# An attention and gated-MLP kernel on one core: the first 180 steps of its hand-written order rearranged

## The chip, the core and the metric

The kernel runs on one core of one Trainium2 chip. A core has five engines that run side by side and meet only at semaphores: TensorE (PE in the profile, with its weight loads as PEld), VectorE (DVE), ScalarE (ACT), GpSimd (POOL) and SyncE (SP). Sixteen DMA engines move data between HBM and the core's memory; SyncE and GpSimd issue the transfers. TensorE writes its results to PSUM, from where VectorE or ScalarE must fetch them. The metric is the device time of one execution in microseconds; less is better.

## The reference

Windowed attention with sink positions (4 batches, 8 heads, 768 positions, head size 64; window 128, 4 sinks), and behind it a gated MLP block on the 512 concatenated features:

```python
scores = scale * np.matmul(q, k.transpose(0, 1, 3, 2))
keep = is_sink | in_window          # pos < 4, or 0 <= i - j < 128
a = softmax(np.where(keep, scores, -1e9))
x = concat_heads(np.matmul(a, v))   # (4, 768, 512)
h = gelu_tanh(x @ w_in)             # 512 -> 1024
u, v = h[..., :512], h[..., 512:]
v_n = (v - mean(v)) / sqrt(var(v) + 1e-6) * g_ln
v_s = einsum('ts,bsd->btd', w_sg, v_n) + b_sg[None, :, None]
out = x + (u * v_s) @ w_out
```

## The kernel before

The four batches go through the same stages, and the stages of neighbouring batches overlap. The order is written out by hand: `STEPS` (lines 20 to 70) is a list of step names, and the loop at line 696 emits them one after another. Each engine runs the instructions it gets from this list strictly in that order. A step that must wait holds up everything behind it on its own engine and nothing on the others. A letter at the end of a step's name says which engine does it: A is ScalarE, D VectorE, P GpSimd, N nobody (the work isn't needed).

The first number of a name is the batch. The steps that matter here, all of batch 0 unless noted:

- LPQ.g, LPK.g (L245 to 253): SyncE loads q or k of two heads (a pair g, 0 to 3) as float32 into tiles that later hold other things (uT and z in the profile's names).
- CPQ.g, CPK.g (L255 to 259, recorded at L200, L201 or L205): cast a pair to bf16.
- TQ, TK (L364 to 377): twelve transposes on TensorE of a pair's q or k into a PSUM tile of the ring mm. EQ, EK (L408 to 432, recorded at L200 or L201): the copy from there to qT or kT.
- QK.0.p.g (L474 to 485): the scores of head pair p and the query blocks 2g and 2g+1, into the ring sc of two tiles. With a 1 at the end, bias matmuls (L479) with -1e9 at the masked places go first, and no mask is needed behind it. EX (L487): exp on ScalarE, from sc to a tile P. MK (L491 to 506): the mask by a multiplication on VectorE, or by two selects on GpSimd; N where the bias was added.
- KS, SK, SX (L450 to 469): the scores of the sinks. KS reads kT of all four pairs.
- LVH.0.0 and LVH.0.1 (L271): GpSimd issues the loads of v for heads 0 to 3 and 4 to 7. ZERO (L347) writes a column of ones into the same tiles beforehand.
- AV.0.p.k (L530 to 554): the products with v for pair p and the query blocks 2k and 2k+1. k = 0 has 6 matmuls, k = 1 and 2 have 10. NR (L556): VectorE divides by the row sums into x_sb, and frees the PSUM tile.
- XT, XE (L565 to 573): transposes of x and their copy to xT. MV, GV, BN, RS, NM, Z (L582 to 621): the half v of the hidden layer, its gelu, statistics and normalised form z. MU, GU: the half u.
- LQ, LK, LW, LWS, LB: further loads that GpSimd issues, of batches 1 and 2 and of the weights. WT, WE: transposes of w_sg and their copy to wsgT.
- SP.0.hf.dc (L644): the products with w_sg, six matmuls that read all of z. GT (L651): VectorE takes their result. VSM (L357), GM (L656) and others stand behind it on VectorE.
- HM.n (L185): n matmuls of zeros (L191) that are put ahead of the next TensorE step which takes a fresh PSUM tile. They keep TensorE busy and compute nothing.

The ring mm has four PSUM tiles, and a step that takes one waits until the copy or division four tiles back has read it. Waits between steps come from the tiles that they share; nothing else sets the order.

Of the kernel before, what the change touches and what calls it, by code (L numbers as in the profile page):

```python
# [17 lines left out]


STEPS = """  # L20
WARM LPQ.0 FILL LPK.0 LPK.1 LPQ.1 LPQ.2 LG MASK LPK.2 LPK.3 CPQ.0.A VSK LPQ.3 IDEN CPK.0.A IDEN2 MASK0 HM.9 TQ.0.0
TK.0.0 EQ.0.0.D EK.0.0.A VSO HM.4 QK.0.0.0 ZERO CPK.1.P QK.0.0.1.1 EX.0.0.0 LVH.0.0 EX.0.0.1 MK.0.0.1.N QK.0.0.2.1
CPQ.1.D TK.0.1 EX.0.0.2 MK.0.0.2.N LC CPQ.2.D LVH.0.1 TQ.0.1 MK.0.0.0.D EK.0.1.A HM.1 TQ.0.2 EQ.0.1.D EQ.0.2.A HM.3
QK.0.1.0 CPK.2.A CPK.3.P QK.0.1.1.1 EX.0.1.0 LQ.1.0 CPQ.3.D TK.0.2 EX.0.1.1 MK.0.1.1.N TK.0.3 EK.0.2.D LQ.1.1 TQ.0.3
EK.0.3.A GTR EQ.0.3.D LW.0 HM.1 QK.0.2.0 QK.0.2.1 EX.0.2.0 LK.1.0 KS.0 VSM.0 HM.3 SK.0.2 EX.0.2.1 SK.0.1 MK.0.2.0.D
AV.0.0.0 LW.1 QK.0.3.0.1 MK.0.1.0.D SX.0.1 SX.0.2 QK.0.3.1 MK.0.2.1.P GCP.D NR.0.0.0 EX.0.3.0 MK.0.3.0.N AV.0.0.1
AV.0.1.0 AV.0.1.1 NR.0.0.1 EX.0.3.1 QK.0.1.2 NR.0.1.0 AV.0.2.0 AV.0.3.0 EX.0.1.2 MK.0.3.1.P NR.0.1.1 QK.0.2.2 AV.0.2.1
NR.0.2.0 EX.0.2.2 TQ.1.0 NR.0.3.0 MK.0.1.2.P QK.0.3.2 AV.0.3.1 EQ.1.0.A NR.0.2.1 XT.0.0 NR.0.3.1 LWS.0 AV.0.0.2
EX.0.3.2 TBL.G.1 AV.0.1.2 XE.0.0.D LK.1.1 XT.0.1 MK.0.2.2.D MV.0.0 XE.0.1.A LK.1.2 NR.0.0.2 MK.0.3.2.D LK.1.3 NR.0.1.2
AV.0.2.2 AV.0.3.2 LQ.1.2 NR.0.2.2 GV.0.0 MV.0.1 NR.0.3.2 LQ.1.3 BN.0.0 LWS.1 XT.0.2 GV.0.1 MU.0.1 XE.0.2.A BN.0.1 WT.0  # L30
GU.0.1 TK.1.0 MV.0.2 LK.1.4 WT.2 EK.1.0.A RS.0.1 LK.1.5 NM.0.1 LB.P LK.2.0 WE.0.D KS.1 GV.0.2 WT.1 MU.0.2 TQ.1.1
LQ.2.0 Z.0.0.D Z.0.3.A Z.0.2.A EQ.1.1.A MU.0.0 WT.5 LQ.2.1 WE.1.D Z.0.1.A BN.0.2 RS.0.2 WE.2.D NM.0.2 GU.0.2 Z.0.4.D
WE.5.D Z.0.5.D TK.1.1 WT.3 EK.1.1.D LQ.1.4 SP.0.0.0 WE.3.D GU.0.0 QK.1.1.0 QK.1.0.0 SP.0.0.2 EX.1.1.0 LQ.1.5 LK.2.1
LVH.1.0 LVH.1.1 GT.0.0.0 TK.1.2 QK.1.2.0 EX.1.0.0 EX.1.2.0 WT.4 GT.0.0.2 SP.0.0.1 EK.1.2.A QK.1.3.0 QK.1.1.1 LQ.2.2
LWO EX.1.3.0 VSM.1 GM.0.0.0.D LK.2.2 GM.0.0.2.P EX.1.1.1 TQ.1.2 WE.4.D SP.0.0.3 TQ.2.0 LK.2.3 QK.1.3.1 LQ.2.3
MK.1.0.0.D GT.0.0.1 MK.1.2.0.D EQ.1.2.A MK.1.3.0.D QK.1.0.1 EX.1.3.1 SP.0.1.1 LQ.2.4 GT.0.0.3 SK.1.0 EX.1.0.1 SX.1.0
LQ.2.5 QK.1.2.1 MK.1.1.1.D MK.1.1.0.D SP.0.1.0 EQ.2.0.D MK.1.3.1.D EX.1.2.1 GM.0.0.3.D TK.2.0 EK.2.0.A GT.0.1.1
QK.1.0.2 QK.1.2.2 SP.0.1.3 GM.0.0.1.D MK.1.0.1.P AV.1.1.0 EX.1.2.2 MK.1.2.1.D GT.0.1.0 GT.0.1.3 LK.2.4 LK.2.5 EX.1.0.2
NR.1.1.0 SP.0.1.2 GT.0.1.2 AV.1.3.0 MK.1.2.2.P QK.1.1.2 NR.1.3.0 AV.1.0.0 OU.0.0 NR.1.0.0 EX.1.1.2 MK.1.0.2.P AV.1.2.0
QK.1.3.2 TK.2.1 MK.1.1.2.P QK.2.1.0 RA.0.0 NR.1.2.0 SN.1.0.1 EX.1.3.2 EX.2.1.0 EK.2.1.D AV.1.0.1 AV.1.2.1 TQ.2.1  # L40
# [695 lines left out]
```

## Time and profile before

| | us |
|---|---|
| median of 3 runs | 155.47 (155.2 to 155.62) |
| the profiled execution | 155.49 |
| its span, first to last instruction | 153.8 |
| TensorE busy | 145.1 |
| VectorE busy | 121.0 |
| GpSimd busy | 103.0 |
| ScalarE busy | 102.9 |

The granted TensorE clock is 1.0 in every slice. A row of the profile names the line, the engine, the operation, what is written from what, the shapes and the count; times are microseconds from the span's start. The list of waits says which engine sat idle before an instruction and what ended it. The chain of waits follows the last instruction back to what released it, step by step. In a row of the order of time, the first number is the start, the second the length.

### The profile page before, as it was taken

What the parts mean: (1) busy time and instruction counts of PE and PEld (TensorE: products, weight loads), DVE (VectorE), ACT (ScalarE), POOL (GpSimd) and SP (SyncE); (2) the same over time, 40 slices, a digit from 0 to 9 for tenths busy, and PEclk for the clock granted to TensorE, in tenths of its full rate; (3) what the DMA queues carried; (4) which work ended last, traced back from release to release, by engine and by line L of the source; (5) the groups of instructions that cost most, each with busy time, mean ns of one, the idle gap of its engine ahead of it and who ended that gap; (6) DMA issues with size and microseconds to landing.
All of it is one profiled execution on the core that took longest, in us unless ns stands there. A gap on an engine that the chain in (4) does not pass through costs nothing.

```text
span 153.8 us, 3859 instructions
## 1 busy us (share of the span) xinstructions
PE 145.1 (94%) x1538; PEld 93.8 (61%) x1554; DVE 121.0 (79%) x291; ACT 102.9 (67%) x119; POOL 103.0 (67%) x134
## 2 busy tenths in 40 slices
PE   6899799999999799999999999999999999999990
PEld 2355476779666577558557664684567644865550
DVE  4677789867899997799969896966889854975982
ACT  3699899588999657767996882578675008597000
POOL 4099689589999979999586947770698900404700
PEclk9999999999999999999999999999999999999999
DMA  4999999999999999999999488999730961064055
GB/s 154 291 376 158 150 197 196 167 188 213 158 150 156 181 152 143 127 150 156 157 216 258 84 272 169 84 231 99 226 119 0 105 124 48 0 205 141 0 205 209
DMA packets 87178, 24.67 MB, mean 160 GB/s; under 512 B 78772, under 2 KB 84920, under 8 KB 87160
## 3 DMA queue, kind: packets, MB, share of 16 engines
q0 software_dynamic: 64608, 11.01, 99.1%
q1 hardware_dynamic: 22552, 13.41, 33.0%
q8 instruction: 12, 0.20, 0.5%
q14 instruction: 6, 0.05, 0.1%
HBM read 24.81 MB, written 6.29 MB: 202 GB/s over the span
## 4 chain that ended last, share of the span: by engine, by line
PE 79%; DMA 9%; DVE 6%; issue 2%; SPq 1%; POOL 1%; DVEq 0%
PE mm L647 18%; PE sc L627 14%; PE sc L586 13%; PE mm L664 13%; DMA v_sb<-in_v_dram 6%; PE sc L484 6%; PE mm L543 5%; DMA uT<-in_k_dram 4%; PE mm L547 3%; DVE P L498 3%; PE mm L383 2%; PE mm L551 1%; DVE gtmp L652 1%; PE mm L639 1%; PE mm L570 1%
## 5 line engine op out<-in xcount | busy, mean ns | idle before, releaser
L489 ACT ACTIVATE P<-sc 128x1024 bf16<-128x1024 f32 (+1 forms) x48 | 43.8, 962 | 11.5 <-PE sc L484 11.0
L647 PE MATMUL mm<-wsgT,z 128*128 128x384 bf16 x192 | 34.5, 326 | 0.9 <-DVE gtmp L652 0.9
L647 PEld LDWEIGHTS <-z 128*128 128x128 bf16 x192 | 17.8, 98 | 12.6 <-issue 1.3
L652 DVE SCALAR_TENSOR_TENSOR gtmp<-mm,g_sb,b_bc 128x384 bf16<-128x384 f32 x32 | 19.1, 611 | 6.1 <-PE mm L647 5.4
L501 POOL TENSOR_SCALAR_AFFINE_SELECT P<-P 128x512 bf16<-128x512 bf16 x23 | 14.9, 648 | 12.7 <-ACT P L489 12.6
L657 POOL TENSOR_TENSOR wsg_gated<-gtmp,uT 128x384 bf16<-128x384 bf16 x18 | 16.5, 931 | 10.1 <-DVE gtmp L652 10.0
L627 PE MATMUL sc<-xT,w_in_sb 128*128 128x256 bf16 x192 | 22.1, 273 | 0.0
L586 PE MATMUL sc<-w_in_sb,xT 128*128 128x512 bf16 x91 | 21.6, 379 | 0.3
L664 PE MATMUL mm<-w_out_sb,wsg_gated 128*128 128x512 bf16 x84 | 21.4, 379 | 0.4
L627 PEld LDWEIGHTS <-w_in_sb 128*128 128x128 bf16 x192 | 18.7, 98 | 3.0
L599 DVE BATCH_NORM_STATS2 st<-vt 128x6 f32<-128x512 f32 x24 | 15.4, 682 | 5.7 <-ACT vt L590 5.6
L561 DVE TENSOR_TENSOR x_sb<-mm,rcp 128x384 bf16<-128x384 f32 (+1 forms) x36 | 18.5, 513 | 1.2
L590 ACT ACTIVATE vt<-sc 128x1024 f32<-128x1024 f32 x12 | 12.3, 1025 | 9.3 <-PE sc L586 9.2
L668 DVE TENSOR_TENSOR ot<-mm,x_sb 128x512 f32<-128x512 f32 x23 | 15.6, 683 | 3.6 <-PE mm L664 3.6
L226 POOL DMA_DIRECT2D k<-in_k_dram x18 | 16.7, 938 | 0.0
L608 POOL TENSOR_TENSOR rs<-rs,neg_half 128x4 f32<-128x4 f32 (+1 forms) x8 | 7.0, 878 | 14.0 <-DVE rs L603 13.1
L226 POOL DMA_DIRECT2D q<-in_q_dram x18 | 16.3, 918 | 0.0
L543 PE MATMUL mm<-v_sb,P 128*128 128x65 bf16 x192 | 15.1, 194 | 1.2 <-DMA v_sb<-in_v_dram 0.8
L543 PEld LDWEIGHTS <-P 128*128 128x128 bf16 x192 | 13.4, 98 | 3.8 <-issue 1.1
L484 PE MATMUL sc<-qT,kT 64*128 64x128 bf16 (+1 forms) x256 | 15.4, 238 | 0.1
L586 PEld LDWEIGHTS <-xT 128*128 128x128 bf16 x96 | 9.3, 98 | 10.3
L504 POOL TENSOR_SCALAR_AFFINE_SELECT P<-P 128x512 bf16<-128x512 bf16 x23 | 15.0, 650 | 0.0
...
## 6 DMA issues: line engine op xcount, KB each, us to landing
...
```

The lines of the kernel that those rows point to most:

```text
L226: return nc.gpsimd.dma_start(out=dst.rearrange("p (h d) -> p h d", h=H), in_=heads(src, b, i))
L484: nc.tensor.matmul(sc[:, hl, c:c + 128 * ni], at(kT, b)[rows, j, p, :], at(qT, b)[rows, i:i + ni, p, :], start=not biased, stop=(not biase ...
L489: nc.scalar.activation(out=P.new((b, p, g))[:, :, 0:w], in_=sc_ring[b, p, g][:, :, 0:w], func=AF.Exp, scale=scale)
L543: nc.tensor.matmul(av[:, il, hl, :], pt[:, hl, c:c + 128], vb[:, h, i, :], start=first, stop=False)
L561: nc.vector.tensor_mul(x_sb.get(b)[:, i0:i0 + n, 128 * p:128 * (p + 1)].rearrange("p t (h d) -> p t h d", h=2), av[:, :, :, 0:Dh], rcp[:, ...
L586: nc.tensor.matmul(hp[:, jl, :], xT[b][:, 2 * g + jl, c, :], w_in_sb[:, c, d_half:2 * d_half], start=(c == 0), stop=(c == KD - 1))
L627: nc.tensor.matmul(hp[:, dc // 2, 256 * (dc % 2):256 * (dc % 2 + 1)], w_in_sb[:, c, 128 * dc:128 * (dc + 1)], xT[b][:, 2 * g:2 * g + 2, c, :],
L647: nc.tensor.matmul(ps[:, 0:NH], z[b][:, si, 128 * dc:128 * (dc + 1)], wsgT[:, si, NH * hf:NH * (hf + 1)], start=(si == 0), stop=(si == NT ...
L652: nc.vector.scalar_tensor_tensor(out=gtmp.new((b, hf, dc)), in0=mm_ring["g", b, hf, dc][:, 0:NH], scalar=g_sb[:, dc:dc + 1], in1=b_bc[:, N ...
L657: (nc.vector if e == "D" else nc.gpsimd).tensor_mul(gated(b, hf)[:, dc, :], gtmp[b, hf, dc], uT[b][:, dc, NH * hf:NH * (hf + 1)])
L664: nc.tensor.matmul(ps, gated(b, hf)[:, dc, 128 * tl:128 * (tl + 1)], w_out_sb[:, dc, :], start=(dc == 0), stop=(dc == KU - 1))
L668: nc.vector.tensor_add(ot.new((b, t)), mm_ring["o", b, t], x_sb[b][:, t, :])
```

## The change

Only the text of `STEPS` changes, and in it only the steps up to the first product with w_sg (SP.0.0.0); from there on the lists are equal. Both hold the same steps of computation. What differs:

- GpSimd's list: LVH.0.0 and LVH.0.1 have no cast ahead of them any more. CPK.2 and CPQ.3 stand between LQ.1.0 and LQ.1.1; before, CPK.1 stood ahead of LVH.0.0 and CPK.3 ahead of LQ.1.0. MK.0.1.2 and MK.0.2.1 leave it and MK.0.3.2 comes. RS.0.2 stands ahead of LQ.2.1 and RS.0.1 behind LK.1.5.
- Casts and copies: CPK.1 and CPQ.1 go to ScalarE, CPK.3 to VectorE, CPK.2 and CPQ.3 to GpSimd. EK.0.0, EK.0.1 and EQ.0.2 go from ScalarE to VectorE, EQ.0.1 to ScalarE.
- Scores: QK.0.0.1 goes ahead of QK.0.0.0. QK.0.3.0 goes ahead of the sink scores and of the first product with v. Biased are QK.0.0.0, 0.0.2, 0.2.1, 0.3.0 and 0.1.2 (before: 0.0.1, 0.0.2, 0.1.1 and 0.3.0).
- Products with v: AV.0.1.0 AV.0.0.0, QK.0.1.2, QK.0.3.1, AV.0.2.0 AV.0.3.0, AV.0.1.1 AV.0.0.1 and so on. Before: AV.0.0.0, QK.0.3.0, QK.0.3.1, AV.0.0.1 AV.0.1.0 AV.0.1.1, QK.0.1.2, AV.0.2.0 AV.0.3.0.
- Warm-up matmuls: 20 instead of 21, at other places.
- Behind that: XE.0.1 and XE.0.2 go from ScalarE to VectorE, Z.0.0 and Z.0.5 the other way, Z.0.2 and EQ.1.1 to VectorE, WE.1 to ScalarE. The transposes WT and TQ.1.1, TK.1.0 stand in another order.

```diff
-WARM LPQ.0 FILL LPK.0 LPK.1 LPQ.1 LPQ.2 LG MASK LPK.2 LPK.3 CPQ.0.A VSK LPQ.3 IDEN CPK.0.A IDEN2 MASK0 HM.9 TQ.0.0
-TK.0.0 EQ.0.0.D EK.0.0.A VSO HM.4 QK.0.0.0 ZERO CPK.1.P QK.0.0.1.1 EX.0.0.0 LVH.0.0 EX.0.0.1 MK.0.0.1.N QK.0.0.2.1
-CPQ.1.D TK.0.1 EX.0.0.2 MK.0.0.2.N LC CPQ.2.D LVH.0.1 TQ.0.1 MK.0.0.0.D EK.0.1.A HM.1 TQ.0.2 EQ.0.1.D EQ.0.2.A HM.3
-QK.0.1.0 CPK.2.A CPK.3.P QK.0.1.1.1 EX.0.1.0 LQ.1.0 CPQ.3.D TK.0.2 EX.0.1.1 MK.0.1.1.N TK.0.3 EK.0.2.D LQ.1.1 TQ.0.3
-EK.0.3.A GTR EQ.0.3.D LW.0 HM.1 QK.0.2.0 QK.0.2.1 EX.0.2.0 LK.1.0 KS.0 VSM.0 HM.3 SK.0.2 EX.0.2.1 SK.0.1 MK.0.2.0.D
-AV.0.0.0 LW.1 QK.0.3.0.1 MK.0.1.0.D SX.0.1 SX.0.2 QK.0.3.1 MK.0.2.1.P GCP.D NR.0.0.0 EX.0.3.0 MK.0.3.0.N AV.0.0.1
-AV.0.1.0 AV.0.1.1 NR.0.0.1 EX.0.3.1 QK.0.1.2 NR.0.1.0 AV.0.2.0 AV.0.3.0 EX.0.1.2 MK.0.3.1.P NR.0.1.1 QK.0.2.2 AV.0.2.1
-NR.0.2.0 EX.0.2.2 TQ.1.0 NR.0.3.0 MK.0.1.2.P QK.0.3.2 AV.0.3.1 EQ.1.0.A NR.0.2.1 XT.0.0 NR.0.3.1 LWS.0 AV.0.0.2
-EX.0.3.2 TBL.G.1 AV.0.1.2 XE.0.0.D LK.1.1 XT.0.1 MK.0.2.2.D MV.0.0 XE.0.1.A LK.1.2 NR.0.0.2 MK.0.3.2.D LK.1.3 NR.0.1.2
-AV.0.2.2 AV.0.3.2 LQ.1.2 NR.0.2.2 GV.0.0 MV.0.1 NR.0.3.2 LQ.1.3 BN.0.0 LWS.1 XT.0.2 GV.0.1 MU.0.1 XE.0.2.A BN.0.1 WT.0
-GU.0.1 TK.1.0 MV.0.2 LK.1.4 WT.2 EK.1.0.A RS.0.1 LK.1.5 NM.0.1 LB.P LK.2.0 WE.0.D KS.1 GV.0.2 WT.1 MU.0.2 TQ.1.1
-LQ.2.0 Z.0.0.D Z.0.3.A Z.0.2.A EQ.1.1.A MU.0.0 WT.5 LQ.2.1 WE.1.D Z.0.1.A BN.0.2 RS.0.2 WE.2.D NM.0.2 GU.0.2 Z.0.4.D
-WE.5.D Z.0.5.D TK.1.1 WT.3 EK.1.1.D LQ.1.4 SP.0.0.0 WE.3.D GU.0.0 QK.1.1.0 QK.1.0.0 SP.0.0.2 EX.1.1.0 LQ.1.5 LK.2.1
-LVH.1.0 LVH.1.1 GT.0.0.0 TK.1.2 QK.1.2.0 EX.1.0.0 EX.1.2.0 WT.4 GT.0.0.2 SP.0.0.1 EK.1.2.A QK.1.3.0 QK.1.1.1 LQ.2.2
-LWO EX.1.3.0 VSM.1 GM.0.0.0.D LK.2.2 GM.0.0.2.P EX.1.1.1 TQ.1.2 WE.4.D SP.0.0.3 TQ.2.0 LK.2.3 QK.1.3.1 LQ.2.3
-MK.1.0.0.D GT.0.0.1 MK.1.2.0.D EQ.1.2.A MK.1.3.0.D QK.1.0.1 EX.1.3.1 SP.0.1.1 LQ.2.4 GT.0.0.3 SK.1.0 EX.1.0.1 SX.1.0
-LQ.2.5 QK.1.2.1 MK.1.1.1.D MK.1.1.0.D SP.0.1.0 EQ.2.0.D MK.1.3.1.D EX.1.2.1 GM.0.0.3.D TK.2.0 EK.2.0.A GT.0.1.1
+WARM LPQ.0 FILL LPK.0 LPK.1 LPQ.1 LPQ.2 LG MASK LPK.2 LPK.3 CPQ.0.A IDEN IDEN2 HM.9 TQ.0.0 MASK0 EQ.0.0.D VSK VSO
+LPQ.3 CPK.0.A ZERO LVH.0.0 HM.3 TK.0.0 LC CPK.1.A EK.0.0.D HM.4 QK.0.0.1 QK.0.0.0.1 EX.0.0.1 LVH.0.1 CPQ.1.A
+MK.0.0.1.D HM.1 TK.0.1 EX.0.0.0 MK.0.0.0.N LQ.1.0 CPK.2.P QK.0.0.2.1 CPQ.3.P EX.0.0.2 CPQ.2.D TQ.0.1 TQ.0.2 TK.0.2
+EQ.0.1.A EK.0.1.D HM.2 QK.0.1.0 LQ.1.1 EQ.0.2.D EX.0.1.0 QK.0.1.1 TQ.0.3 EK.0.2.D CPK.3.D GTR QK.0.2.0 EX.0.1.1
+EX.0.2.0 MK.0.1.0.D LW.0 EQ.0.3.D GCP.D MK.0.1.1.D TK.0.3 EK.0.3.A KS.0 QK.0.2.1.1 EX.0.2.1 QK.0.3.0.1 EX.0.3.0 SK.0.1
+SK.0.2 AV.0.1.0 SX.0.1 MK.0.0.2.N AV.0.0.0 VSM.0 LK.1.0 MK.0.2.0.D QK.0.1.2.1 MK.0.2.1.N SX.0.2 LW.1 QK.0.3.1
+MK.0.3.0.N HM.1 AV.0.2.0 NR.0.1.0 AV.0.3.0 NR.0.0.0 EX.0.3.1 LWS.0 NR.0.2.0 AV.0.1.1 AV.0.0.1 EX.0.1.2 LK.1.1 NR.0.3.0
+TQ.1.0 AV.0.2.1 QK.0.2.2 QK.0.3.2 NR.0.1.1 MK.0.3.1.P AV.0.3.1 NR.0.0.1 NR.0.2.1 NR.0.3.1 XT.0.0 XE.0.0.D EQ.1.0.A
+EX.0.2.2 AV.0.0.2 MK.0.2.2.D MK.0.1.2.N XT.0.1 AV.0.1.2 LK.1.2 MV.0.0 EX.0.3.2 NR.0.1.2 LK.1.3 MK.0.3.2.P NR.0.0.2
+AV.0.2.2 LQ.1.2 LQ.1.3 LWS.1 LK.1.4 TBL.G.1 XE.0.1.D NR.0.2.2 AV.0.3.2 MV.0.1 NR.0.3.2 XT.0.2 GV.0.0 BN.0.0 XE.0.2.D
+MU.0.1 GV.0.1 TK.1.0 BN.0.1 LK.1.5 MV.0.2 GU.0.1 WT.1 RS.0.1 EK.1.0.A NM.0.1 GV.0.2 WE.1.A Z.0.3.A LB.P WT.0 MU.0.2
+Z.0.0.A WT.2 LK.2.0 Z.0.1.A TK.1.1 MU.0.0 TQ.1.1 Z.0.2.D GU.0.2 KS.1 BN.0.2 LQ.2.0 RS.0.2 WE.0.D EK.1.1.D WT.3 WE.2.D
+LQ.2.1 WT.5 NM.0.2 Z.0.5.A Z.0.4.D EQ.1.1.D WE.5.D LQ.1.4 SP.0.0.0 WE.3.D GU.0.0 QK.1.1.0 QK.1.0.0 SP.0.0.2 EX.1.1.0
+LQ.1.5 LK.2.1 LVH.1.0 LVH.1.1 GT.0.0.0 TK.1.2 QK.1.2.0 EX.1.0.0 EX.1.2.0 WT.4 GT.0.0.2 SP.0.0.1 EK.1.2.A QK.1.3.0
+QK.1.1.1 LQ.2.2 LWO EX.1.3.0 VSM.1 GM.0.0.0.D LK.2.2 GM.0.0.2.P EX.1.1.1 TQ.1.2 WE.4.D SP.0.0.3 TQ.2.0 LK.2.3 QK.1.3.1
+LQ.2.3 MK.1.0.0.D GT.0.0.1 MK.1.2.0.D EQ.1.2.A MK.1.3.0.D QK.1.0.1 EX.1.3.1 SP.0.1.1 LQ.2.4 GT.0.0.3 SK.1.0 EX.1.0.1
+SX.1.0 LQ.2.5 QK.1.2.1 MK.1.1.1.D MK.1.1.0.D SP.0.1.0 EQ.2.0.D MK.1.3.1.D EX.1.2.1 GM.0.0.3.D TK.2.0 EK.2.0.A GT.0.1.1
```

## The prediction

> **What bounds the kernel now.** I read the page's head first, then the busy time by stretches, the list of waits of TensorE, and the chain of waits in order of time.
>
> ```profile
> span 153.8 us, 3859 instructions
> PE 145.1 (94%) x1538; PEld 93.8 (61%) x1554; DVE 121.0 (79%) x291; ACT 102.9 (67%) x119; POOL 103.0 (67%) x134
> PE 79%; DMA 9%; DVE 6%; issue 2%; SPq 1%; POOL 1%; DVEq 0%
> ```
>
> The profiled execution took 155.49 us, 1.7 us more than its span; the median of the runs is 155.47, so a sum made on the profile needs no correction. TensorE is busy for 94% of the span, and nine tenths of the chain outside it are a DMA and a stretch of VectorE. The stretches show where there is room at all (columns: PE, PEld, DVE, ACT, POOL busy, clock, DMA, GB/s):
>
> ```profile
> 5.00:17.05 12.05, 10.35 (x156) 5.67 (x157) 8.65 (x19) 10.83 (x15) 9.21 (x10) 1.00 2.04 253
> 17.05:20.00 2.95, 2.53 (x51) 1.81 (x51) 1.83 (x8) 2.19 (x4) 1.20 (x3) 1.00 2.30 175
> 20.00:24.00 4.00, 4.00 (x89) 3.61 (x90) 3.39 (x12) 3.83 (x5) 4.00 (x7) 1.00 1.51 198
> 24.00:38.70 14.70, 14.60 (x156) 11.30 (x156) 11.50 (x34) 12.13 (x15) 12.46 (x15) 1.00 1.73 190
> 41.20:51.20 10.00, 9.07 (x112) 5.97 (x110) 9.93 (x16) 9.97 (x13) 10.00 (x13) 1.00 2.56 161
> 51.20:153.80 102.60, 98.35 (x953) 62.79 (x963) 80.92 (x189) 59.35 (x68) 61.87 (x79) 1.00 1.04 142
> ```
>
> The waits of TensorE between 16.5 and 60 us (total, times, longest):
>
> ```profile
> PE mm L647 <- DVE gtmp L652: 0.9, 1, 0.9
> PE mm L543 <- DMA v_sb<-in_v_dram: 0.8, 1, 0.8
> PE mm L543 <- DVE x_sb L561: 0.4, 1, 0.4
> ```
>
> From 17 to 60 us TensorE waits three times. Two of these waits (0.8 and 0.4) lie in the rewritten part, both at products with v; the third (0.9) ends a stretch in which VectorE is busy for 9.93 of 10.00 us. So after about 20 us every stretch is full on one engine, and what the change does is measured by when TensorE gets from one stretch to the next. The marks of the chain (start, length, what):
>
> ```profile
> 7.40 0.78 POOL k L205
> 8.18 8.87 DMA v_sb<-in_v_dram
> ...
> 17.43 0.32 PE sc L479 x2
> 17.76 0.49 PE sc L484 x10
> ...
> 19.97 0.27 PE mm L543 x3
> ...
> 24.14 0.22 PE sc L586
> ...
> 38.74 0.97 PE mm L647 x6
> ...
> 41.27 0.07 DVE gtmp L652
> ```
>
> The front hangs on v: its first half (LVH.0.0) is issued at 8.18, behind GpSimd's cast of k, and lands at 17.05. The second half:
>
> ```profile
> L272 POOL DMA_DIRECT2D v_sb<-in_v_dram x2: 1417/1614/1812, 8.2 to 10.0; - x2
> ...
> DMA to landing us min/median/max: 8.9/9.4/9.9
> ```
>
> Issued at 10.0, it lands at 19.9, and at 19.97 the first product that needs it (AV.0.2.0) starts.
>
> **The change, part by part.**
>
> *v is issued earlier.* GpSimd no longer casts k's pair 1 ahead of it. LVH.0.0 then waits for ZERO alone, which writes the same tile:
>
> ```profile
> 6.66 0.31 DVE L349 MEMSET v_sb<- 128x48 bf16 x2
> 8.18 3.23 POOL L272 DMA_DIRECT2D v_sb<-in_v_dram  x2
> 11.61 0.82 POOL L205 TENSOR_SCALAR k<-z 128x768 bf16<-128x768 f32 x1 [0.19 <-DMA z<-in_k_dram]
> 12.68 0.99 DVE L201 CAST q<-z 128x768 bf16<-128x768 f32 x1 [1.00 <-DMA z<-in_q_dram]
> ```
>
> That puts the issue at 6.8, 1.3 to 1.4 us earlier. Is v there earlier? The DMA engines over the first 25 us, 40 slices of 0.625 us:
>
> ```profile
> DMA  0008999998999999999999999999999999999999
> GB/s 0 0 0 157 337 383 383 243 241 209 310 359 392 384 399 398 396 340 232 159 179 146 144 149 136 133 128 141 151 173 193 205 207 189 170 195 220 195 214 166
> ```
>
> They are full from 3 us on: with the float32 loads of q and k up to about 11 us (near 400 GB/s), with v behind. An earlier v finds no idle engine; it takes turns with the last q and k loads, and both are done when their sum is done. So v lands between 1.3 us earlier (the engines had room after all) and no earlier; I take no earlier, as the digits are 9 throughout. The last q load (landed 12.65, where the cast at 12.68 starts) is pushed by between 0 and 1.3 us; I take 0.8.
> The Trainium skill, "DMA: Bandwidth & Descriptors", section "Queues, rings and completion order", says that each DMA engine takes turns between the queues that have work for it, a packet at a time. By that rule the issue from another engine buys no bandwidth and the sum is the one below; without it v would come 1.3 us earlier, which is the first rival. The full digits agree with it as far as they go.
>
> *The casts and copies.* SyncE's list keeps its order. The rows of these operations, of the masks behind them on VectorE, and of a mask's half on GpSimd:
>
> ```profile
> 6.43 0.80 ACT L200 COPY kT<-mm 128x768 bf16<-128x768 bf16 x1 [0.65 <-PE mm L377]
> ...
> 8.36 0.56 DVE L201 CAST q<-uT 128x768 bf16<-128x768 f32 x1 [1.27 <-DMA uT<-in_q_dram]
> ...
> 10.28 0.54 DVE L498 TENSOR_TENSOR P<-P,mask 128x768 bf16<-128x768 bf16 x1
> ...
> 13.59 0.94 DVE L201 COPY kT<-mm 128x768 bf16<-128x768 bf16 x1
> ...
> 15.04 1.73 ACT L489 ACTIVATE P<-sc 128x768 bf16<-128x768 f32 x2
> ...
> 23.73 0.68 DVE L498 TENSOR_TENSOR P<-P,mask 128x1024 bf16<-128x1024 bf16 x1
> ...
> L501 POOL TENSOR_SCALAR_AFFINE_SELECT P<-P 128x512 bf16<-128x512 bf16 x23 | 14.9, 648 | 12.7 <-ACT P L489 12.6
> ```
>
> Up to the products with v, VectorE loses the casts of q's pairs 1 and 3 (0.56 and 0.99), a copy of qT (0.94) and a narrow mask (0.54), 3.0 us, and gets two copies of kT and one of qT (0.94 each), a cast of k (as 0.99) and two wide masks (0.68), 5.2 us: 2.2 more, of 3.4 idle in the first stretch above. ScalarE loses four of 0.8 and gets three; GpSimd has two casts (0.82) as before. On the path it does this:
> EK.0.0 moves from ScalarE (6.43 to 7.23) to VectorE behind ZERO: 7.1 to 8.0, so the first scores start 0.8 later. CPQ.1 stands on ScalarE behind EX.0.0.1 and ends at 10.2 instead of 8.92. TensorE's list then waits at TQ.0.3 for CPQ.3, now on GpSimd: landing 12.65 + 0.8, cast 0.82, so 14.3 (13.67 before). Behind it: QK.0.2.0 at 15.0, EX.0.2.0 at 15.4 (15.04 before), EK.0.3.A behind that to 16.9, QK.0.3.0 to 17.35, KS.0 and both SK to 17.8, AV.0.1.0 and AV.0.0.0 to 18.2, QK.0.1.2 with bias to 19.1, QK.0.3.1 to 19.5, one warm-up matmul to 19.7. Then AV.0.2.0 needs v's second half, 19.9. So it starts at 19.97 as now: the lost time of the front is hidden by v, with 0.2 us of cover left. Were the cover gone, each further delay of CPQ.3 would count in full.
>
> *What stands behind v's second half.* Before 19.97 the kernel now computes AV.0.0.1 and AV.0.1.1. The new list has both behind AV.0.3.0, so behind the landing. In their place ahead of it stand scores that were ahead of it already (QK.0.3.0, QK.0.3.1, QK.0.1.2) and time that TensorE waits. The price of the two:
>
> ```profile
> 18.18 0.20 PE L543 MATMUL mm<-v_sb,P 128*128 128x65 bf16 x1
> ...
> 18.56 0.25 PE L543 MATMUL mm<-v_sb,P 128*128 128x65 bf16 x3
> ...
> 18.74 0.19 PE L543 MATMUL mm<-v_sb,P 128*128 128x65 bf16 x1
> ...
> 19.04 0.22 PE L551 MATMUL mm<-v_sink,exs 128*128 128x130 bf16 x1
> ```
>
> AV.0.0.1 runs from 18.18 to 18.56, where AV.0.1.0 starts; AV.0.1.1 from 18.74 to 0.06 behind its last start at 19.04: 0.38 + 0.36 = 0.74 us. All else between AV.0.2.0 and MV.0.0 is the same set, in a stretch where TensorE is busy for 4.00 of 4.00 us. MV.0.0 moves from 24.14 to 24.9.
>
> *Masks and biases.* Five biased scores instead of four, and two masks on GpSimd instead of three. The bias of QK.0.1.2 falls into the time before v's second half, as counted. The mask MK.0.3.1.P follows EX.0.3.1 and ends near 21.9, before AV.0.3.1 (22.9). MK.0.3.2.P (two selects) ends near 25.8, before AV.0.3.2 behind MV.0.0 (26.9). Nothing.
>
> *DMA list of GpSimd.* LQ.1.1 to LW.1 are issued up to 1.1 us later, behind CPQ.3; LWS.0 and LK.1.1 some 4 us earlier, as two masks no longer stand ahead. The order is unchanged, and the queue is far behind its issues (v lands 9 us after its own), so the engines reach none of these before it is issued. Nothing.
>
> *24 to 38.7 us.* Two copies of xT and EQ.1.1 go to VectorE, two z and one wsgT to ScalarE; VectorE gets 0.3 us more of 3.2 idle. TensorE's set is the same, busy for 14.60 of 14.70 us, so SP.0.0.0 moves from 38.74 to 39.5. From there both kernels have the same list. VectorE waits for that product:
>
> ```profile
> 41.27 0.62 DVE L652 SCALAR_TENSOR_TENSOR gtmp<-mm,g_sb,b_bc 128x384 bf16<-128x384 f32 x1 [0.47 <-PE mm L647]
> ```
>
> So its full stretch to 51.2 starts later by the same amount, and TensorE behind it too.
>
> **Sum.** 0 (v) + 0 (front, hidden) + 0.74 (two products behind v) + 0 (the rest) = +0.74 us: 155.49 + 0.74 = 156.2.
>
> **The rivals.**
> - *Not slower: v comes with its issue.* If the engines serve v at once, both halves land up to 1.3 us earlier and the q load isn't pushed, so TQ.0.3 starts 0.8 earlier. Then the two SK end at 17.1, QK.0.3.1 at 18.7, the warm-up at 19.0, and AV.0.2.0 starts there: 19.0 - 19.97 + 0.74 = -0.2, 155.3. It decides from a landing of the second half below 19.2. Against it: the digits of 9. How far it could go is bounded: TensorE has 2.53 + 4.00 + 0.14 us of work from 17.05 to MV.0.0; the move takes out QK.0.3.0 (its bias 0.32, four of the ten in 0.49) and puts in one bias of 512 columns (0.32 x 512/384 = 0.43), so with no wait at all MV.0.0 comes at 17.05 + 6.67 - 0.52 + 0.43 = 23.6 and the time is 155.0.
> - *Slower by more: the q load is late.* If v takes half of the engines from its start, the last q load lands near 14, TQ.0.3 starts at 14.9, and all behind it slips by 0.6; less the cover of 0.2, AV.0.2.0 is 0.4 later, and EX.0.1.2 and EX.0.3.2, which ScalarE takes in turn, hold AV.0.3.1 by as much again at worst: 156.6 to 157.1. For it: ScalarE is busy for 10.83 of 12.05 us in the front already. Against it: the 0.8 are an estimate between the ends.
> - *The reorder hides more than it costs:* QK.0.3.0 ahead of the first product with v fills today's wait of 0.8. That is the edit's plain reading, and true, but the next wait (second half of v) takes it back; it gains only with the first rival.
>
> **How the numbers follow.** The forecast has 0.50 (155.8 to 156.6), the first rival 0.25, the second 0.25. A difference under 0.3% (0.47 us) can't be told from none here. Half of the first rival and the forecast's lower edge are within it, 0.23; faster than 155.0 needs the first rival at its bound or a front shorter than I reckon, 0.17; slower 0.60. The range runs from that bound, 155.0, to the second rival's end with a little above it, 157.2.
>
> **What would show it.** Right: LVH.0.0 issued near 6.8 and landed near 17; its issue-to-landing up from 8.9 to about 10; the last q cast starting past 13; TensorE's wait for v at AV.0.2.0, not at the first product; MV.0.0 at about 24.9, the product with z at 39.5, the VectorE stretch at 42. Wrong: v's second half before 19.2; AV.0.2.0 waiting on ScalarE or VectorE; or a wait in 24 to 38.7, where I have none.

## The result, and the profile after

The changed kernel takes 155.94 us (median of 22 runs) beside 155.31 us for the kernel before on the same chip: a ratio of 1.0039, with a 95% interval of 1.0021 to 1.0057. It is slower by about 0.6 us. (A ratio and its interval leave out executions in a slower state, the medians take in all of them, so the two can differ a little.) The forecast was 156.2 (155.0 to 157.2), with slower as the likeliest. The profiled execution took 155.93 us, 0.44 more than that of before; its span is 154.2 instead of 153.8.

The head of the page of the changed kernel, and its chain by engine:

```profile
span 154.2 us, 3863 instructions
PE 145.0 (94%) x1539; PEld 93.6 (61%) x1555; DVE 122.2 (79%) x293; ACT 100.9 (65%) x117; POOL 102.5 (66%) x132
PE 81%; DMA 7%; DVE 7%; issue 2%; POOL 1%; DVEq 0%
```

TensorE does the same work (145.0 us) in a longer span, so the loss is waiting. Where v was loaded, by the line that issues it (duration of the two issues, their starts, and the time to landing), and all of the DMA engines' packets between 6 and 10.8 us by queue (q1 carries SyncE's loads, q0 those of GpSimd):

```profile
L272 POOL DMA_DIRECT2D v_sb<-in_v_dram x2: 1425/1536/1647, 7.0 to 8.6; - x2
...
DMA to landing us min/median/max: 9.8/10.4/11.0
```

```profile
DMA packets 1242, 1.79 MB, mean 373 GB/s; under 512 B 73, under 2 KB 1242, under 8 KB 1242
## 3 DMA queue, kind: packets, MB, share of 16 engines
q1 hardware_dynamic: 1242, 1.79, 103.2%
```

The issue came 1.2 us earlier (6.98 instead of 8.18), and the time to landing became longer by nearly as much; the landings are at 16.75 and 19.60 instead of 17.05 and 19.92. Not one packet of v moved before 10.84 us; until then the engines, full by their digits, carried SyncE's loads of q and k. These were not done then: from 10.84 to 12.70 us the last 146 packets of q and k (1536 bytes each) moved side by side with those of v. The kernel before has its first packet of v at 11.06.

The marks of the chain in order of time (start, length, what):

```profile
8.63 10.97 DMA v_sb<-in_v_dram
19.60 0.04 issue
...
24.74 0.22 PE sc L586
...
39.34 0.97 PE mm L647 x6
...
41.87 0.04 DVE gtmp L652
```

Every mark behind v is 0.60 us later than before (24.14, 38.74, 41.27). The busy time by stretches (PE, PEld, DVE, ACT, POOL, clock, DMA, GB/s) shows TensorE less busy up to 17.05 us than before (9.82 instead of 10.35), a little more up to 20, and as full as it was behind that:

```profile
5.00:17.05 12.05, 9.82 (x151) 5.22 (x149) 9.23 (x19) 8.99 (x12) 8.70 (x9) 1.00 1.93 255
17.05:20.00 2.95, 2.62 (x51) 1.65 (x52) 1.82 (x6) 2.83 (x5) 2.25 (x3) 1.00 2.32 174
20.00:24.00 4.00, 3.97 (x89) 3.48 (x86) 3.76 (x14) 3.42 (x5) 2.96 (x4) 1.00 1.51 199
24.00:38.70 14.70, 14.60 (x161) 11.32 (x161) 12.10 (x34) 11.40 (x15) 11.68 (x14) 1.00 1.77 194
```

How the 0.60 comes about is read from TensorE's rows in order of time (they start some 0.16 us ahead of the chain's marks, since the chain counts from the end of what was before). Of the kernel before, AV.0.2.0 and MV.0.0:

```profile
19.97 0.27 PE L543 MATMUL mm<-v_sb,P 128*128 128x65 bf16 x3 [0.38 <-DVE x_sb L561]
...
23.98 0.38 PE L586 MATMUL sc<-w_in_sb,xT 128*128 128x512 bf16 x1
```

Of the changed kernel, the same two and a place between them where TensorE stands from 20.38 to 20.51:

```profile
19.64 0.25 PE L543 MATMUL mm<-v_sb,P 128*128 128x65 bf16 x3 [0.18 <-DMA v_sb<-in_v_dram]
...
20.31 0.22 PE L551 MATMUL mm<-v_sink,exs 128*128 128x130 bf16 x1
20.51 0.19 PE L543 MATMUL mm<-v_sb,P 128*128 128x65 bf16 x1
...
24.58 0.38 PE L586 MATMUL sc<-w_in_sb,xT 128*128 128x512 bf16 x1
```

AV.0.2.0 starts 0.33 us earlier, because v lands that much earlier. From there to MV.0.0 it takes 4.94 us instead of 4.01, 0.93 more. Most of this is the two products now behind v's second half. Some 0.25 of it is something else, since the same products between the same marks take 4.67 to 4.72 us in four kernels below (e1, e3, e4, e6): TensorE stops at 20.4 and at 20.9. By the ring each of the two steps needs the PSUM tile of a product four tiles back, and VectorE's divisions, which free these tiles, run late. Why they do stands in VectorE's rows of the changed kernel:

```profile
16.91 0.19 DVE L451 TENSOR_TENSOR ks_sink<-kT,halfsel 128x32 bf16<-128x32 bf16 x1 [0.17 <-ACT kT L200]
18.20 0.69 DVE L358 TENSOR_TENSOR v_sink<-vs,headsel 128x512 bf16<-128x512 f32 x1 [1.10 <-DMA vs<-in_v_dram]
18.81 0.55 DVE L498 TENSOR_TENSOR P<-P,mask 128x768 bf16<-128x768 bf16 x1
19.28 0.17 DVE L560 RECIPROCAL rcp<-mm 128x4 f32<-128x4 f32 x1
```

VSM.0 waits 1.10 us for the sink rows of v (four transfers of 8 KB that SyncE issues), and the first division, at 17.47 in the kernel before, comes at 19.28. In the kernel before VSM.0 ran at 15.41 without a wait: the last packet of those rows moved at 12.9; here it moved at 16.68 and the rows were there at 18.08. This differs between executions: in e2 and e4 below, whose front is the same, the last packets moved at 14.98 and 15.19.

From the product with w_sg (SP.0.0.0) to the end it is the other way round. In the chain, the product before the turn of the divisions near 87 us and the one behind it, first of the kernel before, then of the changed kernel:

```profile
85.41 0.97 PE mm L647 x6
...
89.97 1.95 PE mm L647 x12
```

```profile
86.00 0.98 PE mm L647 x6
...
90.31 1.79 PE mm L647 x11
```

The delay is 0.59 at the first and 0.34 at the second, so some 0.25 is given back within 4 us, although both lists are equal there. In the end 0.4 of the 0.6 is left in the span.

### The profile page after: what moved, and what is told of

Its sections match the earlier page's. It is cut to its first block, busy times and chain, and to the rows that moved or that the text cites. A ratio compares the mean times of both kernels' runs of the same rounds, so it can differ in the third digit from the quotient of the medians.

```text
span 154.2 us, 3863 instructions
## 1 busy us (share of the span) xinstructions
PE 145.0 (94%) x1539; PEld 93.6 (61%) x1555; DVE 122.2 (79%) x293; ACT 100.9 (65%) x117; POOL 102.5 (66%) x132
## 4 chain that ended last, share of the span: by engine, by line
PE 81%; DMA 7%; DVE 7%; issue 2%; POOL 1%; DVEq 0%
PE mm L647 18%; PE sc L627 14%; PE sc L586 13%; PE mm L664 13%; DMA v_sb<-in_v_dram 7%; PE sc L484 5%; PE mm L543 4%; PE mm L547 3%; PE mm L383 3%; DVE P L498 3%; PE mm L191 2%; PE mm L551 1%; DVE gtmp L652 1%; PE mm L639 1%; POOL v_sb L272 1%
## 5 line engine op out<-in xcount | busy, mean ns | idle before, releaser
L647 PEld LDWEIGHTS <-z 128*128 128x128 bf16 x192 | 17.8, 98 | 12.6 <-issue 1.3
L652 DVE SCALAR_TENSOR_TENSOR gtmp<-mm,g_sb,b_bc 128x384 bf16<-128x384 f32 x32 | 19.2, 612 | 6.6 <-PE mm L647 6.3
L501 POOL TENSOR_SCALAR_AFFINE_SELECT P<-P 128x512 bf16<-128x512 bf16 x22 | 14.5, 657 | 13.1 <-ACT P L489 13.0
L657 POOL TENSOR_TENSOR wsg_gated<-gtmp,uT 128x384 bf16<-128x384 bf16 x18 | 16.5, 932 | 9.7 <-DVE gtmp L652 9.6
L599 DVE BATCH_NORM_STATS2 st<-vt 128x6 f32<-128x512 f32 x24 | 15.4, 683 | 5.8 <-ACT vt L590 5.8
L226 POOL DMA_DIRECT2D q<-in_q_dram x18 | 16.8, 945 | 0.0
L632 ACT ACTIVATE uT<-sc 128x1024 bf16<-128x1024 f32 x12 | 12.1, 1016 | 4.0 <-PE sc L627 3.9
```

What stands on the lines that cost most here:

```text
L226: return nc.gpsimd.dma_start(out=dst.rearrange("p (h d) -> p h d", h=H), in_=heads(src, b, i))
L647: nc.tensor.matmul(ps[:, 0:NH], z[b][:, si, 128 * dc:128 * (dc + 1)], wsgT[:, si, NH * hf:NH * (hf + 1)], start=(si == 0), stop=(si == NT ...
L652: nc.vector.scalar_tensor_tensor(out=gtmp.new((b, hf, dc)), in0=mm_ring["g", b, hf, dc][:, 0:NH], scalar=g_sb[:, dc:dc + 1], in1=b_bc[:, N ...
L657: (nc.vector if e == "D" else nc.gpsimd).tensor_mul(gated(b, hf)[:, dc, :], gtmp[b, hf, dc], uT[b][:, dc, NH * hf:NH * (hf + 1)])
```

## The experiments

All eleven beside the two kernels, in one table. The landing of v's second half and the starts of MV.0.0 and SP.0.0.0 are from each one's profiled execution (order of time); the last column is its span less SP.0.0.0. One profiled execution scatters: the last load of q lands between 12.6 and 13.9 us in these executions, and v's second half between 18.98 and 20.25. So the marks show how a kernel works, and the ratios, from 6 runs (e3) to 22, what it is worth.

| kernel | ratio to before (95%) | v's 2nd half | MV.0.0 | SP.0.0.0 | SP to end |
|---|---|---|---|---|---|
| before | 1 | 19.92 | 23.98 | 38.57 | 115.2 |
| changed | 1.0039 (1.0021 to 1.0057) | 19.60 | 24.58 | 39.17 | 115.0 |
| e1 products alone | 1.0082 (1.0051 to 1.0113) | 19.76 | 24.52 | 39.11 | 115.2 |
| e2 products back | 1.0024 (0.9990 to 1.0057) | 19.06 | 23.66 | 38.26 | 114.9 |
| e3 v late | 1.0117 (1.0068 to 1.0167) | 19.86 | 25.91 | 40.50 | 114.9 |
| e4 sink later | 1.0056 (1.0026 to 1.0086) | 19.18 | 24.19 | 38.78 | 114.9 |
| e5 scores alone | 1.0001 (0.9966 to 1.0037) | 19.49 | 23.66 | 38.25 | 115.2 |
| e6 more cover | 1.0075 (1.0048 to 1.0103) | 19.71 | 25.26 | 39.85 | 115.0 |
| e7 two scores | 0.9980 (0.9949 to 1.0011) | 19.02 | 23.54 | 38.14 | 115.2 |
| e8 two scores and tail | 1.0067 (1.0033 to 1.0101) | 18.98 | 23.17 | 38.85 | 114.9 |
| e9 tail alone | 1.0069 (1.0033 to 1.0105) | 20.25 | 24.31 | 39.69 | 115.1 |
| e10 tail, mask back | 1.0012 (0.9975 to 1.0048) | 19.97 | 23.60 | 38.56 | 114.9 |
| e11 two scores again | 1.0007 (0.9969 to 1.0044) | 19.60 | 24.19 | 38.79 | 115.3 |

**e1: the two products alone.** The kernel before, with AV.0.0.1 and AV.0.1.1 (and their divisions) behind AV.0.3.0:

```diff
-AV.0.0.1 AV.0.1.0 AV.0.1.1 NR.0.0.1 EX.0.3.1 QK.0.1.2 NR.0.1.0 AV.0.2.0 AV.0.3.0 EX.0.1.2 MK.0.3.1.P
+AV.0.1.0 EX.0.3.1 QK.0.1.2 NR.0.1.0 AV.0.2.0 AV.0.3.0 EX.0.1.2 AV.0.0.1 AV.0.1.1 MK.0.3.1.P
...
```

> The kernel before with one part of the change: AV.0.0.1 and AV.0.1.1 (and their divisions) moved behind AV.0.3.0; casts, masks, scores and loads stay as they were. If the two products behind v's second half are what the change costs, AV.0.2.0 still starts at v's landing (19.9), MV.0.0 slips from 24.14 by 0.5 to 0.75 us, and the time rises by as much, 0.3 to 0.5%. If the cost comes from the casts and copies of the front, this is the kernel before, within 0.2 us.

Measured: 156.06 us beside 155.19, slower by 0.82%. The waits of TensorE between 16.5 and 60 us (the row of v; before it was the wait for the first half):

```profile
PE mm L647 <- DVE gtmp L652: 0.9, 1, 0.9
PE mm L543 <- DMA v_sb<-in_v_dram: 0.6, 1, 0.6
```

AV.0.2.0 starts at 19.80, the moment v's second half is there, after a wait of 0.6 us. From AV.0.2.0 to MV.0.0 it takes 4.72 us instead of 4.01: 0.71 for the two products, where the forecast had 0.74. So this one edit alone makes a loss of at least the changed kernel's size. The timed loss, by the ratio 1.27 us with an interval from 0.8 to 1.8, is even larger than the 0.7 and than the 0.3% to 0.5% expected; the profiled execution doesn't show the rest, and it stays open.

**e2: the two products back.** The changed kernel, with the two ahead of AV.0.2.0 again, in the place of the warm-up matmul:

```diff
-MK.0.3.0.N HM.1 AV.0.2.0 NR.0.1.0 AV.0.3.0 NR.0.0.0 EX.0.3.1 LWS.0 NR.0.2.0 AV.0.1.1 AV.0.0.1 EX.0.1.2
+MK.0.3.0.N AV.0.1.1 AV.0.0.1 NR.0.1.0 AV.0.2.0 NR.0.0.0 AV.0.3.0 EX.0.3.1 LWS.0 NR.0.1.1 NR.0.0.1 EX.0.1.2
...
```

> The changed kernel with that part undone: AV.0.1.1 and AV.0.0.1 stand ahead of AV.0.2.0, in the time in which TensorE waits for v's second half, and the warm-up matmul there is taken out. By the forecast's term this takes back most of the loss: products start at 19.1, AV.0.2.0 at 19.9, MV.0.0 at 24.2 to 24.3 instead of 24.74, time 0.4 to 0.6 us less than the changed kernel, level with the kernel before. If the late sink rows (VSM.0, which ends at 18.9) and the divisions behind them are the true limit, the divisions still follow one another from 19.3 and MV.0.0 stays above 24.5.

Measured: 155.48 us, 0.24% above the kernel before, with an interval that holds no change. That is 0.15% below the changed kernel, in the direction expected, but too little to be told apart, so the times alone don't show that undoing the step undoes the loss. The trace does show the step: from AV.0.2.0 (19.53) to MV.0.0 (23.66) it takes 4.13 us, where the kernels with the products behind v take at least 4.67. These 0.54 us, 0.35% of the time, lie inside the interval. The profile also shows what sets AV.0.2.0 once the products fill the gap: its wait for v is gone, and the front (casts, transposes, scores) comes last instead, nearly as late as in the changed kernel (QK.0.3.1 starts at 18.26; there at 18.53). This would explain why the products behind v cost less in the changed kernel than in e1: a part of the room that they leave is taken by its later front. It was not tried by itself.

**e3: v issued late.** The changed kernel, with one more cast on GpSimd ahead of LVH.0.0, as CPK.1 stood there before. It writes the tile wsg_gated, whose content is overwritten later, so it adds work and changes no result.

```diff
-LPQ.3 CPK.0.A ZERO LVH.0.0 HM.3
+LPQ.3 CPK.0.A ZERO DUM LVH.0.0 HM.3
```

> The changed kernel with a cast on GpSimd ahead of LVH.0.0 that waits for the same load as the old cast and writes to a place that is overwritten later: v is issued at 8.2 again instead of 7.0. If the DMA engines are full anyway, v's landings move back by 0.3 us only (17.05 and 19.9), the last q load lands near 12.7 again instead of 13.44, and the sink rows come in time, so VSM.0 no longer waits 1.1 us; the time changes by less than 0.3 us either way. If v really profits from its earlier issue, it lands 1.2 us later than in the changed kernel (18.0 and 20.8) and the time rises by 1 us.

Measured: slower by 1.17%, the most of all, where less than 0.3 us was expected. GpSimd's rows, and the wait of TensorE that follows from them (L380 is the line of the changed kernel's L377 here):

```profile
8.39 0.83 POOL L342 TENSOR_SCALAR wsg_gated<-uT 128x768 bf16<-128x768 f32 x1 [4.79 <-DMA uT<-in_k_dram]
9.18 3.44 POOL L272 DMA_DIRECT2D v_sb<-in_v_dram  x2
12.60 0.88 POOL L226 DMA_DIRECT2D q<-in_q_dram  x1
13.50 0.85 POOL L205 TENSOR_SCALAR k<-z 128x768 bf16<-128x768 f32 x1
14.30 0.84 POOL L205 TENSOR_SCALAR q<-z 128x768 bf16<-128x768 f32 x1
```

```profile
PE mm L380 <- POOL k L205: 2.0, 1, 2.0
```

v was issued 2.2 us later than in the changed kernel and landed at the same time: 16.75 (16.75) and 19.86 (19.60). So an early issue doesn't bring v early; that part of the forecast stands. What the edit costs is GpSimd's time: its cast of k's pair 2 moves from 11.32 to 13.50, and TensorE waits 2.0 us at TK.0.2. The front, by the start of the warm-up matmul ahead of AV.0.2.0, then is 1.93 us later than in the changed kernel (21.01 instead of 19.08), AV.0.2.0 is 1.60 later (21.24), since 0.33 of cover was left, and MV.0.0 is 1.33 later, since the divisions now are in time. So a front beyond its cover counts in full, as the second rival had it. (The cover is 0.33 by starts: AV.0.2.0 follows the warm-up matmul after 0.23 us here and after 0.56 in the changed kernel, where it waits for v. The 0.18 in the row of the changed kernel count from the modelled end of that matmul.) The edit delays v's issue and GpSimd's casts together, and it is the casts that the trace shows on the path. The last load of q landed at 13.54 here, with v's first packet 0.7 us later than in the changed kernel (13.44). So its lateness against the 12.65 of before is not shown to be the doing of an early v, as the forecast had it; e5, a form of the kernel before that issues v at 8.83, has 13.51.

**e4: VSM.0 behind two divisions.** The changed kernel, without its wait for the sink rows ahead of the divisions:

```diff
-AV.0.0.0 VSM.0 LK.1.0 ... AV.0.3.0 NR.0.0.0 EX.0.3.1
+AV.0.0.0 LK.1.0 ... AV.0.3.0 NR.0.0.0 VSM.0 EX.0.3.1
```

> The changed kernel with VSM.0, which waits 1.1 us for the sink rows, moved on VectorE from ahead of the mask MK.0.2.0 and the first two divisions to behind them. If that wait holds the divisions and through them TensorE's tiles, NR.0.1.0 starts at 18.1 instead of 19.28, TensorE's short stops at 20.4 and 21.0 go, MV.0.0 comes 0.15 to 0.3 us earlier and the time falls by as much. If the two products alone set it, MV.0.0 stays at 24.7.

Measured: 155.66 us, a ratio of 1.0056, not different from the changed kernel's. The trace does show the stops gone. VectorE's first division comes at 18.23, VSM.0 behind it without a wait:

```profile
18.23 0.18 DVE L560 RECIPROCAL rcp<-mm 128x4 f32<-128x4 f32 x1 [0.36 <-PE mm L547]
...
19.33 0.68 DVE L358 TENSOR_TENSOR v_sink<-vs,headsel 128x512 bf16<-128x512 f32 x1
```

From AV.0.2.0 (19.51) to MV.0.0 (24.19) it takes 4.68 us instead of 4.94. So the wait for the sink rows is worth some 0.25 us in the profiled execution of the changed kernel. The times, expected to fall by as much, didn't; this fits with a wait that is not always there: in e2, with VSM.0 in its old place, VSM.0 ran at 16.91 without one.

**e5: the scores alone.** The kernel before, with QK.0.3.0 ahead of the first product with v:

```diff
-SK.0.1 MK.0.2.0.D AV.0.0.0 LW.1 QK.0.3.0.1 MK.0.1.0.D
+SK.0.1 QK.0.3.0.1 MK.0.2.0.D AV.0.0.0 LW.1 MK.0.1.0.D
```

> The kernel before with the other part of the change alone: QK.0.3.0 (with its bias) moved ahead of the first product with v, into TensorE's wait for v's first half; the order of the products, the casts and the loads stay. By the forecast's third rival TensorE's wait at the first product shrinks from 0.8 to about 0.2 us and the wait at AV.0.2.0, for v's second half, grows by the same 0.5 to 0.6: time within 0.2 us of the kernel before. If scores ahead are worth something by themselves, AV.0.2.0 starts earlier than v's landing in the kernel before allowed and the time falls by 0.5 us.

Measured: 155.31 beside 155.32, no difference (the interval goes from 0.34% faster to 0.37% slower). TensorE's wait of 0.8 us for v's first half is gone from its waits, and nothing was gained. The forecast had it that the next wait, for v's second half, would grow by as much. This trace doesn't show that: it has no wait there either. TensorE goes from QK.0.1.2 straight on to AV.0.2.0:

```profile
19.32 0.40 PE L484 MATMUL sc<-qT,kT 64*128 64x256 bf16 x6
19.64 0.27 PE L543 MATMUL mm<-v_sb,P 128*128 128x65 bf16 x3
```

v's second half had landed at 19.49. In this execution the front itself is later (TQ.0.3 at 14.48 instead of 13.72, behind a load of q that landed at 13.51 instead of 12.65), and it took the room of the wait. So that the scores ahead are worth nothing alone is measured; that the wait for v's second half is what takes them back is not shown.

**e6: four more warm-up matmuls ahead of AV.0.2.0.** They compute nothing, and take the place of the cover:

```diff
-MK.0.3.0.N HM.1 AV.0.2.0 NR.0.1.0
+MK.0.3.0.N HM.5 AV.0.2.0 NR.0.1.0
```

> The changed kernel with five warm-up matmuls instead of one ahead of AV.0.2.0: 0.86 us of TensorE time more, at the place where it waits for v's second half. In the changed kernel 0.2 us of wait were left there. If the start of AV.0.2.0 passes to the end in full, as the forecast has it, MV.0.0 moves from 24.6 by 0.86 - 0.2 = 0.66 us and the time rises by 0.6 to 0.7 (0.4%) over the changed kernel, to 0.8% over the kernel before. If the stretches behind have room, less than half of it is left at the end.

Measured: slower by 0.75% than before, 0.36% than the changed kernel. The rows of the warm-up and of AV.0.2.0:

```profile
19.50 1.25 PE L191 MATMUL mm<-warm 128*128 128x512 bf16 x5
20.59 0.26 PE L543 MATMUL mm<-v_sb,P 128*128 128x65 bf16 x3
```

The front ahead of them ends 0.42 later in this execution, and the four matmuls add 0.86; less the cover of 0.33, AV.0.2.0 comes 0.95 later. MV.0.0 comes 0.68 later, because the divisions then are in time (4.67 us between the two). The cover is nearly as thin as the forecast's 0.2: what is added to the front shows in the time.

**e7 and e11: the next wait filled too.** e5 with QK.0.2.2 ahead of AV.0.2.0, measured twice:

```diff
-SK.0.1 MK.0.2.0.D AV.0.0.0 LW.1 QK.0.3.0.1 MK.0.1.0.D
+SK.0.1 QK.0.3.0.1 MK.0.2.0.D AV.0.0.0 LW.1 MK.0.1.0.D
...
-QK.0.1.2 NR.0.1.0 AV.0.2.0 AV.0.3.0 EX.0.1.2 MK.0.3.1.P NR.0.1.1 QK.0.2.2 AV.0.2.1
+QK.0.1.2 NR.0.1.0 QK.0.2.2 AV.0.2.0 AV.0.3.0 EX.0.1.2 MK.0.3.1.P NR.0.1.1 AV.0.2.1
```

> The kernel before with QK.0.3.0 ahead of the first product with v, and in the time that this frees ahead of v's second half another score that stood behind it, QK.0.2.2 (0.33 us); the products keep their places. By the theory that work moved from behind the landing of v's second half to ahead of it is what counts, MV.0.0 comes 0.33 us earlier and the time falls by 0.3 us (0.2%). If ScalarE, whose exponential of QK.0.3.1 must free the tile first, comes too late, TensorE waits there instead and nothing is gained.

> The kernel before with QK.0.3.0 (biased) ahead of the first product with v and QK.0.2.2 ahead of AV.0.2.0, measured once more, since its ratio of 0.998 had an interval that took in 1. My theory: MV.0.0 0.3 to 0.4 us earlier than before and nothing lost behind it, ratio 0.997 to 0.999. Rival: the scores do nothing and the first measurement was scatter of the loads; ratio 1.000 to 1.002.

Measured: 0.9980 the first time, 1.0007 the second; both intervals hold 1. Neither trace has a wait for v left. In the first, v landed at 19.02 and MV.0.0 came at 23.54; in the second the last load of q landed at 13.51 instead of 12.91, and MV.0.0 came at 24.19. With both waits for v filled, the front is next, and it goes with the loads of q. Nothing is shown to be gained.

**e8, e9 and e10: the later part of the list.** e8 is e7 and e9 the kernel before, each with the changed kernel's list from XT.0.0 on; e10 is e8 with the mask of QK.0.3.2 on VectorE again (MK.0.3.2.D for MK.0.3.2.P).

```diff
-XT.0.0 NR.0.3.1 LWS.0 AV.0.0.2 EX.0.3.2 TBL.G.1 AV.0.1.2 XE.0.0.D LK.1.1 XT.0.1 MK.0.2.2.D MV.0.0 XE.0.1.A LK.1.2 NR.0.0.2 MK.0.3.2.D
+XT.0.0 NR.0.3.1 LWS.0 LK.1.1 XE.0.0.D AV.0.0.2 MK.0.2.2.D XT.0.1 AV.0.1.2 LK.1.2 MV.0.0 EX.0.3.2 NR.0.1.2 LK.1.3 MK.0.3.2.P
...
```

> The kernel before with QK.0.3.0 (biased) ahead of the first product with v and QK.0.2.2 ahead of AV.0.2.0 (as in the run with two scores), and from XT.0.0 on the changed kernel's list. My theory: the rearranged casts behind XT.0.0 are worth nothing up to SP.0.0.0 (14.6 us from MV.0.0 in both kernels) and 0.2 to 0.25 us somewhere behind it, so MV.0.0 stands near 23.6 as in that run, and the time is 155.0 - 0.2 = about 154.8 us, 0.3% to 0.4% under the kernel before. Rival, that the 0.2 us given back at 87 us in the changed kernel belong to its later start there and not to its list: time as in that run, about 155.0 us, and 129.8 us from MV.0.0 to the end as in the kernel before.

> The kernel before with the changed kernel's list from XT.0.0 on and nothing else. My theory: MV.0.0 stays near 24.1 us and from there to the end it is 129.5 us instead of 129.8: about 155.2 us, 0.1% to 0.2% faster, within what can be told apart only by the marks. Rival, that the gift depends on the later start: 129.8 us behind MV.0.0 and the time of the kernel before. A third: the casts moved there cost something between 24 and 38.7 us; then SP.0.0.0 comes more than 14.6 us behind MV.0.0.

> The kernel with two scores moved and the changed kernel's list from XT.0.0 on, with one letter back: MK.0.3.2 is a multiplication on VectorE again, as in the kernel before. In the run with GpSimd's two selects they stood behind two masks and four DMA issues and ended at 26.3 us, and AV.0.3.2 waited for them; SP.0.0.0 came 15.7 us behind MV.0.0 instead of 14.6. My theory: that wait was the whole loss of 1.1 us, so SP.0.0.0 comes 14.6 to 14.8 us behind MV.0.0 and the end 115.0 us behind SP.0.0.0: about 154.8 us, 0.2% to 0.4% under the kernel before. Rival: VectorE, 11.2 of 14.7 us busy there, has no room for the mask beside two more copies; then SP.0.0.0 comes over 15 us behind MV.0.0 and the time is 155.3 us or more.

Measured: e8 and e9 are slower by 0.7%. e8 was expected to be 0.3% to 0.4% faster, so that failed; for e9 the third case came true, the one in which the later list costs something. The chain of e8 shows why:

```profile
21.68 0.71 POOL wsg_gated L283
22.39 2.66 POOL k L226 x3
25.06 0.66 POOL P L501
25.71 0.60 POOL P L504
26.31 0.05 issue
26.36 0.20 PE mm L547
```

The mask's two selects stand on GpSimd behind four DMA issues (0.71 and 2.66 us), which stand behind two earlier masks. They end at 26.3, and AV.0.3.2 waits; SP.0.0.0 comes 15.7 us (e8) and 15.4 us (e9) behind MV.0.0 instead of 14.6. In the changed kernel the same mask on GpSimd costs nothing: GpSimd has only one mask ahead of it instead of three (QK.0.1.2 is biased there, so MK.0.1.2 isn't needed, and MK.0.2.1 is gone too), and then waits 1.38 us for the exponential. e2, with MV.0.0 at 23.66, has the same list and no wait of TensorE either. So, as the traces read, the parts of the change hang together; no run moves these biases by themselves. That the later list alone is a loss is measured. With the mask on VectorE (e10), SP.0.0.0 comes 15.0 us behind MV.0.0 and the time is 1.0012 of before, with an interval that holds no change: by the marks most of the loss is gone. What the trace shows of the rest is a wait of TensorE of 0.7 us for a division, where VectorE has the mask as well. Each of its two theories is half right. No version of these is shown to beat the kernel before.

The last column of the table tells the gift at 87 us apart. With the later list of before it is 115.2 to 115.3 us from SP.0.0.0 to the end (five kernels, SP.0.0.0 from 38.14 to 39.11), with the changed one's 114.9 to 115.1 (eight kernels, from 38.26 to 40.50). It goes with the list ahead of SP.0.0.0, not with how late the product comes. Why an equal list behind it then runs 0.2 us shorter stays open: near 87 us, VectorE in the kernel before shows a wait for scores that the changed kernel doesn't have.

```profile
86.84 0.62 DVE L652 SCALAR_TENSOR_TENSOR gtmp<-mm,g_sb,b_bc 128x384 bf16<-128x384 f32 x1 [0.47 <-PE sc L484]
```

```profile
87.09 0.62 DVE L652 SCALAR_TENSOR_TENSOR gtmp<-mm,g_sb,b_bc 128x384 bf16<-128x384 f32 x1
```

The same wait, 0.47 to 0.48 us, stands in all five kernels with the later list of before and in none of the eight others. What makes it was not tried.

## Why the prediction was right, and where it was not

The term that the forecast rests on, two products behind v's second half, is shown by e1 and by the stretch from AV.0.2.0 to MV.0.0: 4.01 to 4.13 us with the two ahead of it (before, e2, e5), 4.67 to 4.94 with the two in it (the changed kernel, e1, e3, e4, e6). That the total came as near as it did is in part luck: three things that the sum doesn't have, v's earlier landing, the late divisions and the gift at 87 us, partly cancel.

- *v is issued earlier* (forecast: issued at 6.8, landing no earlier): right. Issued at 6.98, landed 0.3 earlier; e3 shows that 2.2 us at the issue are nothing at the landing. The first rival's bound, a second half ahead of 19.2, was not reached by the changed kernel (19.60). The Trainium skill, "DMA: Bandwidth & Descriptors", section "Queues, rings and completion order", has the engines take turns between queues that have work; this trace agrees from 10.84 us on, where the packets of both queues move side by side. It doesn't show it for the 3.9 us ahead of that, in which no packet of v moved; whether v's packets were ready to take a turn in that time is not to be seen. The landing came out near what the forecast took by that rule.
- *The last q load is pushed by 0.8*: the number was right (13.44 instead of 12.65), the cause is not shown, since e3 and e5 have the same without an early v. This hit may be luck.
- *Casts and copies* (TQ.0.3 at 14.3, warm-up to 19.7, cover 0.2): right. TQ.0.3 started at 14.39, the warm-up ended at 19.47, and AV.0.2.0 then waited 0.18 for v (0.33 if counted by starts, see e3). TensorE's wait of 0.8 us at TK.0.2 for GpSimd's cast of k, which the forecast didn't have, cost nothing, since the one at TQ.0.3 behind it came last. Missed was VSM.0 on VectorE: the sum has no wait for its rows of v, whose four loads SyncE issues behind the last one of q, and they came at 18.08. In the changed kernel's trace this cost some 0.25 us behind AV.0.2.0; e4 shows no price of it in the times.
- *What stands behind v's second half* (+0.74): right, 0.66 to 0.71 by the same stretch in e1, e3, e4 and e6. With v 0.33 earlier and the divisions' 0.25 it makes the +0.60 of MV.0.0.
- *Masks, GpSimd's DMA list, 24 to 38.7 us* (nothing): right for the change as a whole (14.6 us from MV.0.0 to SP.0.0.0 in both), but not free in itself: behind the kernel before's masks and DMA issues the mask on GpSimd costs 0.8 to 1.1 us (e8, e9).
- *All of it reaches the end*: right to 51 us, where the delay is 0.62; then 0.2 of it is given back near 87 us. The step "from there both kernels have the same list" didn't say that equal lists can run differently.
- *Rivals*: the reorder that hides more than it costs gains nothing that the times show (e5, e7, e11), but the reason given, the next wait, is not what e5's trace shows; a late front does cost in full (e3, e6), but here the front was in time by 0.18 to 0.33 us.
- *A reading of the profile*: the DMA (9%) and VectorE (6%) are 15 of the 21% of the chain outside TensorE, seven tenths and not nine. Nothing in the sum rests on it.

The measured 0.39% (0.6 us) stands beside the forecast's 0.74 us. In the two profiled executions the sum is 0.74, less v's 0.33, less the 0.2 at 87 us, plus the divisions' 0.25, which makes 0.46 beside their difference of 0.44. v's landing and the divisions scatter between executions, so this is not a sum for the medians.
